# A written-out order of 2,098 parts drawn anew, and two of eight products of a matrix multiplication put last

## The chip, the cores and the metric

The kernel runs on one core of a Trainium2 chip. The metric is the device time of one execution in microseconds (us). The engines are PE (TensorE, matrix products), DVE (VectorE), ACT (ScalarE), POOL (GpSimd) and SP (SyncE); each works through its own queue of instructions in order. SP computes nothing here: it issues every transfer (DMA) of the kernel, one after the other, and waits at the head of its queue until the data of the next transfer are ready.

## The reference, cut to what matters

```python
for t in range(S):                       # S = 768, 4 batches, 8 heads, D = 40
    y[:, :, t] = einsum('bhd,bhde->bhe', r_t, state)
    Sa = einsum('bhde,bhe->bhd', state, a_t)
    state = state * w_t[:, :, None, :] - einsum('bhd,bhe->bhde', Sa, b_t) \
            + einsum('bhd,bhe->bhde', v_t, k_t)
x = y.transpose(0, 2, 1, 3).reshape(4, 768, 320)
h = maximum(x @ w_in, 0)                 # w_in: 320 x 1024
conv_out[t] = sum(conv_w[k] * h[t + k - 1] for k in range(3))
out = (h * sigmoid(conv_out)) @ w_out    # w_out: 1024 x 320
```

A recurrence over 768 time steps makes y; a product with w_in, a convolution over three time steps, a gate and a product with w_out follow.

## The kernel before

The recurrence is solved in 24 chain steps of 32 time steps each. Two chain steps form a pair, whose inputs w, a, k, b and r are loaded together; v is loaded for each step. The output goes through the second part in 12 windows of 64 time steps. The work of every step, pair and window is written as Python generators, cut by `yield` into parts, and the string `ORDER` names the parts one by one: `advance` runs a part up to its next `yield`, and so the order of the string is the order in which each engine gets its instructions. Nothing reorders them afterwards. What stands first in an engine's queue and waits holds up all that stands behind it on that engine.

The parts that matter here, by the names of their tiles (a number behind a name counts steps or pairs, for xh and xl it is the first step of the window):

- `solve_in` (pair): SP stores at, the scores of the pair, as bd in DRAM and reads it back as bb.
- `solve` (pair): 15 pairs of small operations on POOL make xx from bb (for pair 0 on DVE). SP stores xx as xd, then reads xd back as tt, and bd once more as nb. For the first two pairs SP first fills xd with zeros.
- `chain` (step): on PE pp, then pw (reads tt), pe (reads nb), pu (reads tt) and pn; between them ACT and DVE bring the results back. DVE makes the new state s, POOL makes se from it, and pp of the next step reads se.
- `finish` (step): PE turns the output (pq), DVE makes xf, ACT makes xh, POOL makes xl, the rest that xh left of xf. The 320 columns stand as three groups of 120, 120 and 80 rows, so the third group leaves 40 of 120 rows free.
- `moe_pack` (window): two transfers that move rows of xh into the free rows of the third group, of xh and of xl. `move_rows` does the same once for the weights wih and wil, and ACT then copies 80 rows of wih into wil.
- `moe_in` (window and quarter fp): for each of two column blocks j, eight products into ph; then the convolution and gate on ACT and DVE, which leave g.
- `moe_out`: po, the product of g with the weights wo.
- `weights`: 23 pieces of the weights, in 64 bits each, are loaded and changed to 32 bits by five operations on DVE and one or two each on ACT and POOL.

The eight products of a block stand in this order before (`wih[:, 2]`, `wil[:, 2]`, `xh[:, 2]` and `xl[:, 2]` hold moved rows):

```python
passes = (
    (wih[:, 0], xh[:, 0]), (wih[:, 1], xh[:, 1]), (wih[:, 2], xh[:, 2]),
    (wil[:, 0], xh[:, 0]), (wil[:, 1], xh[:, 1]), (wih[:, 0], xl[:, 0]),
    (wih[:, 1], xl[:, 1]), (wil[:, 2], xl[:, 2]),
)
```

Of the kernel before, what the change touches and what calls it, by code (L numbers as in the profile page):

```python
# [40 lines left out]
    pa0 we6 ou0 we6 we3 pa0 ch1 dd2.0 we5 ut0 we7 ut0 lv0 ut0 ch1 ld2 we7 ha3 de2.0 lr0 ha3 dd2.0
    ld3 ch1 si0 we6 lv0 so1 dd2.0 we6 ld2 so1 we8 ha3 sc2 dd2.1 so0 ch1 sc4 dd2.1 fi0 we8 ch1 dd2.1
    ch1 sc4 ch1 lr1 sc5 ut1*2 st1 lv2 pa1 ou1 dd2.0 we8 lv2 we7*2 we9*2 fi0 sc5 we8 ou1 fi0 ld3
    de3.0 lr1 we9 ch2 we10 we9 we11 we10 so1 ch2 ou1 si1 we9 we11 fi1 rt1 lv3 we10 fi1 si2 we11 ch2
    lv3 we11 fi1 we10*2 so2 si2 rt1 we12 st2 sc1 ha4 we13 de3.0 ch2 we12 ch2 we13 ld3 we8 ou2 ch2
    ut2 ch2 ut2 dd3.0 ld3 we13 we12 pa2 sc4 ou2 so2 we12 we13 we14 we15 we14 ha4 ha5 ld3 ha4 ha5 ou2
    we15 ha5 we14 dd3.0 fi2 ch3 st3 we14 ch3 dd3.0 we16 lv4 so2 we15 we16*2 de3.1 so2 ro0 we6 we15
    we17 ch3*2 lv4 ha2 de3.1 fi2 we17 ch3 fi2 so1 lr2 we17 we16 de3.1 we18 dd3.1*3 we16 ut3*2 ch3
    pa3 ch3 ld4 we18*2 we17 dd1.1 ou3 ro0 pk0 mi0.0 we19 ld4 pk0 we18*3 sc6 lr2 ou3 ro0 we17 we11
    we20 we19 sc6 sc7 we18 de4.0 fi3 so2 we19 ch4 we12 we19 mi0.0 we19 ch4 st4 lv5 mi0.0 we20 mi0.1  # L50
    we20*2 rt0 we21 we22 ld4 rt2 sc7 we17 we20 ch4 we21 we20 mi0.1 we20 rt2 mi0.0 dd1.0 ch4 de4.0
    lv5 fi3 si3 we22 fi3 ou4 ch4 de4.1 ch4*2 we19 ut4 we21 we7 so3 ut4 mi0.0 ha6 pa4 mi0.1 ou4 ld4
    ld5 pa4 de1.0 we17 mi0.2 si3 ou0 ch2 mi0.0*2 ld4 so3 ha6 mi0.1 fi3 mi0.1 ut2 mi0.0 mi0.2 mi0.0
    mi0.2 rt2 ou0 mi0.0 mi0.2 ch5 so3 lr3 ch5 ha7 sc6 so3 mi0.1 dd4.0 ha7 lv5 mo0.0 dd4.0 we19 st5
    de4.1 lr3 ch1 dd4.0 lr1 mi0.1 ch0 ch5 mi0.2 mi0.3 dd4.1*2 ch5 mi0.1*2 we21 mi0.3 dd2.1 ch1 de5.0
    mi0.3 ou5 mi0.2 ch4 we4 ch5 pk1 fi4 mi1.0 sc8 ut3 ut5 mi0.1 lv6 ld5 mi0.2*3 ld5 mi1.0 mo0.0
    de4.1 mi0.2 ch5 lv6 fi4 mi0.3 ut5 dd4.1 mi1.0 mi0.3 pa5 sc8 we5 so3 lv6 ou5 mi0.3 mi1.1 fi4 fi5
    ld5 fi4 sc9 ut4 ha8 rt3 lv1 mi0.3 sc9 st2 st1 fi5 fi4 ch5 mi0.3 ch6*2 st6 de5.0 mi0.3 mi1.0
# [93 lines left out]
def tile_decay_delta_attention_then_conv_gate_moe(  # L152
# [136 lines left out]
    wih = cp.tile([GR, G, DF], F32R, name="wih")  # L289
# [886 lines left out]
```

## Time and profile before

| what | value |
|---|---|
| time, median of 3 runs | 607.12 us (604.34 to 611.71) |
| the profiled execution | 608.01 us, of which the span of its instructions 606.3 us |
| mean granted clock of PE | 0.947 of full speed |
| PE busy | 539.3 us, 89% of the span |
| DVE, ACT, POOL busy | 395.9, 384.9 and 323.8 us |

The span runs from the first to the last instruction; 1.7 us of the execution lie outside it. PE has two clocks, 2.4 GHz (granted clock 1.00) and 1.2 GHz (0.50); a mean between them says which share of a stretch ran at which. "Issue" as the cause of a wait means that the profile shows nothing that the engine waited for.

### The profile page before, as it was taken

The page shows a single profiled execution, that of the slowest core. Times are in us where ns is not written, and L with a number is a line of the kernel's source. Part 1 is how long each engine was busy: PE and PEld are TensorE (multiplying, and loading weights), DVE is VectorE, ACT ScalarE, POOL GpSimd, SP SyncE. Part 2 cuts the span into 40 slices and gives each one's busy share as a digit, 9 for nine tenths or more (in the row PEclk, how much of TensorE's full clock was granted, in tenths as well). Part 3 has the DMA queues.
Part 4 walks back from the last instruction along what each step waited for, and adds up shares of the span by engine and source line. Part 5 has one row for each costly group of instructions (what it writes and reads, how often), then busy time and mean ns, then how long its engine had stood idle before and what let it go on. Part 6 is the DMA issues. An engine that isn't in the chain of part 4 may idle for free.

```text
span 606.3 us, 29431 instructions
## 1 busy us (share of the span) xinstructions
PE 539.3 (89%) x13021; PEld 450.5 (74%) x13021; DVE 395.9 (65%) x757; ACT 384.9 (63%) x922; POOL 323.8 (53%) x690
## 2 busy tenths in 40 slices
PE   3666776798989999989699999999999999899998
PEld 2555565686878788778588878788788887787884
DVE  7897788998796566638366476566556743654660
ACT  2354366576886776666568676857677666576561
POOL 4414886976858638556408637347538457330000
PEclk9967697898999999999989999999899999899999
DMA  9955845667345463442451357334431231200001
GB/s 149 151 108 100 153 104 113 148 133 118 64 94 87 87 119 56 87 84 45 90 89 36 65 98 130 73 69 71 90 68 36 65 54 30 58 6 27 23 27 35
DMA packets 214755, 49.11 MB, mean 81 GB/s; under 512 B 203324, under 2 KB 208404, under 8 KB 214628
## 3 DMA queue, kind: packets, MB, share of 16 engines
q1 hardware_dynamic: 214628, 47.23, 41.3%
q8 instruction: 102, 1.67, 1.2%
q14 instruction: 25, 0.20, 0.1%
HBM read 36.72 MB, written 9.18 MB: 76 GB/s over the span
## 4 chain that ended last, share of the span: by engine, by line
PE 61%; DVE 13%; ACT 10%; DMA 8%; issue 3%; POOL 3%; SPq 2%; DVEq 0%; POOLq 0%; ACTq 0%
PE po L934 15%; PE ph L889 12%; PE pm L534 3%; PE pn L724 3%; ACT vu L712 3%; PE pu L705 3%; PE ps L534 2%; PE pp L669 2%; DVE cc L918 2%; DMA bd<-at 2%; PE py L837 2%; PE pvt L787 2%; DMA xh<-xh 2%; PE pw L681 2%; PE pp L657 2%
## 5 line engine op out<-in xcount | busy, mean ns | idle before, releaser
L918 DVE SCALAR_TENSOR_TENSOR cc<-hb,cw,cc 128x256 f32<-128x256 f32 x192 | 111.3, 601 | 16.2 <-ACT cc L910 12.7
L934 PE MATMUL po<-wo,g 128*128 128x320 f32 x384 | 117.4, 443 | 0.0
L748 POOL TENSOR_TENSOR se<-s,ws 120x480 f32<-120x480 f32 x69 | 72.1, 1073 | 47.7 <-DVE s L739 29.3
L934 PEld LDWEIGHTS po<-wo,g 128*128 128x128 f32 x384 | 68.9, 192 | 22.3 <-issue 0.8
L622 POOL TENSOR_TENSOR stg<-xx,bb 128x15 f32<-128x15 f32 (+4 forms) x165 | 55.9, 339 | 27.7 <-DMA bb<-bd 16.4
L889 PE MATMUL ph<-xh,wih 120*128 120x256 f32 x288 | 57.3, 306 | 7.4 <-DMA xh<-xh 7.4
L739 DVE SCALAR_TENSOR_TENSOR s<-pn,side,s 120x240 f32<-120x240 f32 x90 | 35.8, 460 | 42.6 <-PE pn L724 42.6
L628 POOL TENSOR_TENSOR xx<-xx,stg 128x15 f32<-128x15 f32 (+4 forms) x165 | 53.4, 324 | 12.9
L712 ACT COPY vu<-pu 32x320 f32<-32x320 f32 x96 | 40.1, 418 | 23.2 <-PE pu L705 21.5
L926 DVE TENSOR_TENSOR g<-cc,hb 128x512 f32<-128x512 f32 x48 | 36.1, 755 | 23.3 <-ACT cc L923 23.3
L865 POOL TENSOR_TENSOR xl<-xf,xh 120x384 fp32r<-120x384 f32 x24 | 26.0, 1084 | 45.6 <-ACT xh L863 45.6
L889 PEld LDWEIGHTS ph<-xh,wih 120*128 120x128 f32 x288 | 41.4, 191 | 11.2 <-DMA xh<-xh 7.8
L910 ACT ACTIVATE cc<-hb,cw 128x256 f32<-128x256 f32 x96 | 43.8, 509 | 0.9 <-POOL hb L899 0.9
L800 ACT ACTIVATE sn<-pt,hmask 120x480 f32<-120x480 f32 x69 | 40.7, 665 | 3.5 <-PE pt L797 3.3
L903 ACT ACTIVATE hb<-ph 128x512 f32<-128x512 f32 x48 | 28.7, 599 | 21.1 <-PE ph L889 21.0
L923 ACT ACTIVATE cc<-cc 128x512 f32<-128x512 f32 x48 | 30.3, 635 | 17.8 <-DVE cc L918 17.7
L889 PE MATMUL ph<-xl,wih 120*128 120x256 f32 x192 | 39.0, 284 | 2.0 <-issue 2.0
L558 ACT ACTIVATE ap<-ah,hmask 120x384 f32<-120x384 f32 (+1 forms) x72 | 36.5, 574 | 6.5 <-DVE ah L513 6.4
L889 PE MATMUL ph<-xh,wil 120*128 120x256 f32 x192 | 38.7, 283 | 0.0
L493 POOL TENSOR_TENSOR ws<-wc,hmask 120x18 f32<-120x18 f32 x24 | 5.9, 247 | 59.2 <-DVE wc L489 58.9
L424 POOL COPY vu<-vin 96x240 f32<-96x240 f32 (+1 forms) x72 | 29.8, 451 | 12.7 <-DMA vin<-in_v_dram 10.6
L855 DVE TENSOR_TENSOR xf<-pq,pre 120x384 f32<-120x384 f32 x24 | 13.3, 553 | 33.1 <-PE pq L853 29.7
(310 smaller groups left out, 1281.2 us busy)
## 6 DMA issues: line engine op xcount, KB each, us to landing
inw<-in_w_dram SPq DMA_DIRECT2D x24, 160.0 KB
ina<-in_a_dram SPq DMA_DIRECT2D x24, 160.0 KB
ink<-in_k_dram SPq DMA_DIRECT2D x24, 160.0 KB
inb<-in_b_dram SPq DMA_DIRECT2D x24, 160.0 KB
rin<-in_r_dram SPq DMA_DIRECT2D x24, 160.0 KB
vin<-in_v_dram SPq DMA_DIRECT2D x48, 80.0 KB
out_dram<-ob SPq DMA_DIRECT2D x22, 160.0 KB
bd<-at SPq DMA_DIRECT2D x24, 128.0 KB
```

Of the source, the lines that this page charges most:

```text
L558: nc.scalar.activation(out=ap[:, by_set(h)], in_=ah[:, : NH[h]], func=AF.Copy, scale=hmask[:, h : h + 1])
L622: eng.tensor_tensor(t3, xx[:, 0:nj, i : i + 1].to_broadcast([128, nj, nt]), bb[:, i : i + 1, i + 1 :].to_broadcast([128, nj, nt]), ALU.mult,)
L628: eng.tensor_tensor(xx[:, 0:nj, i + 1 :], xx[:, 0:nj, i + 1 :], t3, ALU.add)
L712: nc.scalar.copy(vu[q, y, :HD], pu[y][q])
L739: nc.vector.scalar_tensor_tensor(out=dst, in0=src, scalar=side[:, x : x + 1], in1=dst if x else old[:, zs], op0=ALU.mult, op1=ALU.add,)
L748: nc.gpsimd.tensor_tensor(wide.rearrange("p b g h d -> p (b g) h d")[:, :, h], new.rearrange("p b g d -> p (b g) d"), ws[:, :, h : h + 1]. ...
L800: nc.scalar.activation(out=sn.rearrange("p b h g d -> p (b h) g d")[:, :, g], in_=pt[:GR].rearrange("p b (h d) -> p (b h) d", d=D), func=A ...
L889: nc.tensor.matmul(ph[:, j], l[:, fs], x, start=(j == 0 and i == 0), stop=(i == len(passes) - 1), skip_group_check=True,)
L910: nc.scalar.activation(out=cc[:, j], in_=hb[:, j, :, 1 : W + 1], func=AF.Copy, scale=cw[:, 1, f : f + 1],)
L918: nc.vector.scalar_tensor_tensor(out=cc[:, j], in0=hb[:, j, :, x : W + x], scalar=cw[:, x, f : f + 1], in1=cc[:, j], op0=ALU.mult, op1=ALU ...
L926: nc.vector.tensor_tensor(gt, cc, hb[:, :, :, 1 : W + 1], ALU.mult)
L934: nc.tensor.matmul(po[:rows, :DM], part(f), wo[:, f, :], start=(f == 0), stop=(f == NF - 1))
```

## The change

The string `ORDER` is replaced: the same parts in the same number, in another order, which was drawn by a planner that counts the transfers as a queue that serves one after the other. In `moe_in` the two products with moved rows come last of the eight. No operation is added or removed; the sums into ph are added up in another order. Lines behind the table are higher by one.

```diff
 ORDER = """
-    ld0*2 de0.0*2 de0.1*2 dd0.0 ld0 dd0.0 ld0 dd0.0 dd0.1 ld0 de0.0 de0.1 dd0.0 dd0.1*2 sc0 lr0*2
+    ld0 de0.0*2 de0.1 ld0 de0.0 de0.1 ld0*2 dd0.0*2 ld0 dd0.0 dd0.1 dd0.0 dd0.1 sc0 dd0.1 we0*2
...
@@ -877,9 +878,9 @@
         passes = (
-            (wih[:, 0], xh[:, 0]), (wih[:, 1], xh[:, 1]), (wih[:, 2], xh[:, 2]),
-            (wil[:, 0], xh[:, 0]), (wil[:, 1], xh[:, 1]), (wih[:, 0], xl[:, 0]),
-            (wih[:, 1], xl[:, 1]), (wil[:, 2], xl[:, 2]),
+            (wih[:, 0], xh[:, 0]), (wih[:, 1], xh[:, 1]), (wil[:, 0], xh[:, 0]),
+            (wil[:, 1], xh[:, 1]), (wih[:, 0], xl[:, 0]), (wih[:, 1], xl[:, 1]),
+            (wih[:, 2], xh[:, 2]), (wil[:, 2], xl[:, 2]),
         )
```

Three places show what the new table does. The first is SP's queue at the start, from the read of tt0 for chain step 0 on (ina, ink, inb and inw are the inputs of the next pair, wi02r and wi12r pieces of the weights). Before:

```order
L636 DMA tt0_564<-xd0_140 128x1x512
L640 DMA nb0_566<-bd0_321 128x1x512
L415 DMA ina_126<-in_a_dram 64x16x40 x2
L590 DMA xd1_141<-zero_138 1024x1x64
L595 DMA bd1_695<-at2_509 32x1024 x2
L604 DMA bb1_698<-bd1_695 64x16x16 x2
L415 DMA ink_128<-in_k_dram 64x16x40 x2
L365 DMA wi02r_845<-in_moe_w_in_dram 120x512
L365 DMA wi12r_908<-in_moe_w_in_dram 120x512
```

And in the change:

```order
L637 DMA tt0_597<-xd0_140 128x1x512
L641 DMA nb0_599<-bd0_325 128x1x512
L591 DMA xd1_141<-zero_138 1024x1x64
L596 DMA bd1_738<-at2_534 32x1024 x2
L605 DMA bb1_741<-bd1_738 64x16x16 x2
L366 DMA wi02r_828<-in_moe_w_in_dram 120x512
L366 DMA wi12r_844<-in_moe_w_in_dram 120x512
L416 DMA ina_126<-in_a_dram 64x16x40 x2
L416 DMA ink_128<-in_k_dram 64x16x40 x2
```

The load of ina has moved from ahead of the zeros and bd1 to behind both pieces of the weights, and these now come ahead of ink.

The second place is SP's queue around the moved rows of window 4 (xh8 and xl8), which stand near the solution of pair 6 (xx6, tt6, nb6). Before:

```order
L444 DMA rin_132<-in_r_dram 64x16x40 x2
L432 DMA vin_136<-in_v_dram 32x16x40 x2
L634 DMA xd0_140<-xx6_5186 64x16x16 x2
L636 DMA tt6_5785<-xd0_140 128x1x512
L640 DMA nb6_5787<-bd6_5044 128x1x512
L432 DMA vin_136<-in_v_dram 32x16x40 x2
L959 DMA out_0_dram<-ob20_5647 2x64x320
L873 DMA xh8_4868<-xh8_4868 40x256
L873 DMA xl8_4869<-xh8_4868 40x256
```

And in the change:

```order
L445 DMA rin_132<-in_r_dram 64x16x40 x2
L416 DMA inw_124<-in_w_dram 64x16x40 x2
L416 DMA ina_126<-in_a_dram 64x16x40 x2
L433 DMA vin_136<-in_v_dram 32x16x40 x2
L874 DMA xh8_4859<-xh8_4859 40x256
L874 DMA xl8_4860<-xh8_4859 40x256
L635 DMA xd0_140<-xx6_5047 64x16x16 x2
L637 DMA tt6_5878<-xd0_140 128x1x512
L641 DMA nb6_5880<-bd6_5036 128x1x512
```

The moved rows stand ahead of xd, tt6 and nb6 now, and behind two loads that came later before. Those of window 3 (xh6) move in the same way, from behind bb6 to ahead of the solution of pair 5.

The third place is PE's queue in chain step 3, at the first product of the second part (ph00). Before:

```order
L461 MATMUL pw31_1884<-ident_80,inw_124 120x128 x3
L681 MATMUL pw3_1904<-psb3_1853,tt1_1363 32x40 x32
L692 MATMUL pe3_1939<-w13_1937,nb1_1365 32x40 x32
L705 MATMUL pu30_1991<-psb3_1853,tt1_1363 32x40
L705 MATMUL pu31_1992<-psb3_1853,tt1_1363 32x40
```

And in the change:

```order
L682 MATMUL pw3_1892<-psb3_1881,tt1_1348 32x40 x32
L693 MATMUL pe3_1937<-w13_1925,nb1_1350 32x40 x32
L890 MATMUL ph00_1982<-xh0_1041,wih_152 128x256 x2
L890 MATMUL ph00_1982<-xh0_1041,wil_153 128x256 x2
L890 MATMUL ph00_1982<-xl0_1042,wih_152 128x256 x2
L890 MATMUL ph00_1982<-xh0_1041,wih_152 128x256
L890 MATMUL ph00_1982<-xl0_1042,wil_153 128x256
L706 MATMUL pu30_1991<-psb3_1881,tt1_1348 32x40
```

The eight products of the first block of window 0 stand between pe3 and pu3 now; before they came behind most of step 3. The transfers of window 0's moved rows have moved up in SP's queue as well, to right behind `move_rows`.

## Rows read from the trace of the kernel before

**Rows 1.** The page, part 1: busy time, share of the span and instructions.

```profile
PE 539.3 (89%) x13021; PEld 450.5 (74%) x13021; DVE 395.9 (65%) x757; ACT 384.9 (63%) x922; POOL 323.8 (53%) x690
```

**Rows 2.** Windows: length, busy time of each engine, granted clock, DMA share.

```profile
0.00:150.00 150.00, 103.43 (x2604) 87.91 (x2605) 124.72 (x262) 80.01 (x186) 92.81 (x206) 0.83 0.69 128
150.00:606.30 456.30, 435.84 (x10420) 362.60 (x10417) 271.21 (x496) 304.88 (x737) 231.01 (x485) 0.99 0.34 66
```

**Rows 3.** Waits of PE from 150 us: total, times, longest.

```profile
PE ph L889 <- DMA xh<-xh: 7.4, 2, 5.6
PE pp L669 <- issue: 2.8, 3, 1.3
PE ph L889 <- issue: 2.0, 1, 2.0
...
PE pe L692 <- ACT w L686: 0.2, 1, 0.2
```

**Rows 4.** Timeline of PE, the two products that waited for moved rows.

```profile
264.57 0.39 PE L889 MATMUL ph<-xh,wih 120*128 120x256 f32 x1 [1.82 <-DMA xh<-xh]
...
302.93 0.58 PE L889 MATMUL ph<-xh,wih 120*128 120x256 f32 x1 [5.56 <-DMA xh<-xh]
```

**Rows 5.** Timeline of SP's queue of transfers around the longer of these waits.

```profile
289.68 0.60 SPq L636 DMA_DIRECT2D tt<-xd  x1
...
293.59 4.42 SPq L873 DMA_DIRECT2D xh<-xh  x1
```

**Rows 6.** Chain of waits: the two transfers that ended them (start, duration).

```profile
262.16 2.36 DMA xh<-xh
...
293.59 9.30 DMA xh<-xh
```

**Rows 7.** Windows of the longer wait and of the stretch behind it.

```profile
297.30:303.00 5.70, 0.14 (x2) 0.07 (x1) 1.08 (x3) 0.63 (x1) 1.93 (x4) 0.80 0.47 105
303.00:307.50 4.50, 4.50 (x76) 3.79 (x77) 0.77 (x2) 1.23 (x3) 0.00 (x0) 0.50 0.94 151
```

**Rows 8.** Chain of waits at the start: start, duration, what.

```profile
41.51 0.64 SPq L415
...
43.95 4.75 SPq L590
...
48.80 0.60 SPq L595
...
49.44 5.02 DMA bd<-at
...
61.87 2.94 POOL se L748 x3
```

**Rows 9.** Timeline of DVE at the start: source of bd1, wait for weights.

```profile
44.30 1.28 DVE L567 TENSOR_TENSOR at<-ps,trin 128x512 f32<-128x512 f32 x2
...
62.92 1.03 DVE L300 TENSOR_SCALAR wi02q<-wi02r 120x256 int32<-120x256 int32 x1 [3.00 <-DMA wi02r<-in_moe_w_in_dram]
```

**Rows 10.** Timeline of PE, the last two products of chain step 3's solve.

```profile
114.53 0.79 PE L692 MATMUL pe<-w,nb 32*32 32x40 f32 x64 [0.70 <-ACT w L686]
116.96 1.64 PE L705 MATMUL pu<-psb,tt 32*32 32x40 f32 x64 [1.63 <-DVE psb L696]
```

**Rows 11.** Timeline of SP's queue: moved rows of weights and of window 0.

```profile
106.10 0.91 SPq L373 DMA_DIRECT2D wih<-wil  x1
...
115.24 3.02 SPq L873 DMA_DIRECT2D xh<-xh  x1
```

**Rows 12.** Window of low clock around chain step 3.

```profile
116.40:123.20 6.80, 6.22 (x111) 5.60 (x115) 6.33 (x14) 3.27 (x8) 6.17 (x17) 0.50 0.76 142
```

**Rows 13.** Chain of waits: one group of eight products at full clock.

```profile
266.26 1.13 PE ph L889 x8
```

**Rows 14.** Waits of SP's queue over the whole span.

```profile
SPq L873 <- POOL xl L865: 36.2, 2, 23.2
```

**Rows 15.** Timeline of PE: the product of step 12 that reads tt6.

```profile
309.55 0.79 PE L681 MATMUL pw<-psb,tt 32*32 32x40 f32 x64
```

More of the change, by code (lines that the diff above doesn't have):

```diff
@@ L41 @@
[L41 to L46, printed above, removed]
@@ new lines @@
+    de0.1 sc0 sc1 sc0 sc1 lv0 we1 lv0 we0*2 we1 ld1 we2 de1.0 we2 ld1 de1.0 ld1 we0 si0 so0 dd1.0
+    si0 we1 ha0*2 so0*2 we1 we2 lr0 lv0 ha1 de1.1 lr0 we3 we2 ha1 so0 we1 dd1.0 ld1 ld2 de1.1 ld1
+    ch0*2 dd1.0 lv1 dd1.1 we4 dd1.1 lr0 dd0.1 rt0 ha1 dd1.1 lv1 we3 we4 ha0 sc2*2 sc3 de2.0 de1.0
+    sc3 we3*2 we5 we4 ha2 de2.0 so0 we2 sc2 ch0 we5 ch0 de2.1 ch0 we4 we3 de2.0 de2.1 rt0 si1 ch0
+    so1 ut0*2 ha2 pa0 ch0 si1 we5 we6 so1 we5 we7 dd1.0 ou0*2 ha3 pa0 ou0 we6 ch1 ut0 we7 ut0 ch1
+    ha3 so1 ld2 ou0 ch1 we6*3 so1 ld2*2 dd2.0*2 ld2 we7 rt0 dd2.0 dd2.1 we5 fi0 pa0 ch1 lr1 we8 we7
@@ new lines @@
+    ch6 lv6 lv7 de5.0 ou6 mi1.0 de5.1 ch6 mo0.0 so3 ld5 lv7 de5.1 ha8 ut6 sc7 ut6 ch6 lv7 st1 ld5
+    pa6 mi1.1 pa6 ou6 ha9*2 mi0.3 ut6 dd5.0*2 dd5.1 fi1 dd5.0 ut6 lr3 si4 mi1.1 de5.1 mi1.1 ha9
+    dd5.1 mi1.2 mi1.0 so4 fi5 pa6 si4 ch6 ch7 sc10 fi4 ou6 lv1 mi1.0 mi1.2 we21 mo0.0 ch0 fi5 ch7
+    mi1.2 ch7 dd5.1 ch6*2 st7 mi1.0 ut6 mi1.3 ch4 lr4 mi1.1 lv8 ou6 ld6 de6.0 lv6 lr4 ch7 lv8 mo0.1
+    mi1.2 mi1.1 ld6 mi1.2 mi0.2 ch7 mi1.1 mi1.3 mi1.1 lr4 fi3 mi1.3 fi5 mi1.2 ha8 ch6 mi1.3 lv8
+    mi1.2 fi6 so4 mi1.0 ld6 mi1.1 ut7*2 dd3.0 mi1.1 lv9 ch7 sc10 sc11 sc10 pa7 sc11 fi6 ou7 lr1 ou7
@@ new lines @@
+    fi13 ch14 ut14 mi4.2 ut14 mi5.0 mi4.2 lv16 mi5.0*2 ch14 mi4.3 ha14 pa14 mi5.1 mi5.0 ld9 mi4.3
+    mi5.1*2 fi12 mi4.3 sc17 ld9 ha16 lv16 ut14 ou14 mi5.0 ch15 pa3 ch15 ha17*2 so8 lv15 ch14 mi4.3
+    dd9.0*2 mi5.0 mi5.1 dd9.1 lv16 mi4.2 lv17 mi5.2 mo3.0 mi5.0 mi5.2 mi5.0 lv16 st15 so8 mo3.1
+    dd9.1 ch14 mi5.1 ch15 mi5.1 st7 mo4.0*2 ld9 ch14 ch15 mi5.2 ch15 dd9.0 mi5.0 sc18 mi5.3 mi5.1
+    ch15 mi5.2 ut15 mi5.1 mi5.3 mi5.1 so8 mi5.1 ha17 ch13 ut15 ou15 ld10 st2 mi5.3 lv17 fi14 rt8
+    dd9.1 ch15*2 pa15 sc18 ou15 mi5.2 ld10 ch13 ch16 ha18 so8 lr1 sc19 ld10 mi5.2 de10.0 ch16 fi14
@@ new lines @@
+    mo4.0 mo3.1 st6 ld10 lv17 ou15 lv18 mi5.3 mo4.0 sc3 ou15 ch16 mi5.3 fi14 st16 fi15 lv3 ch16
+    mo4.1 de10.0 we22 de6.1 sc18 rt8 so8 mo4.1 ch16 mi5.3 mo4.1 ch16 ut16*2 pk6 mi6.0 fi14 ha16 fi14
+    mi5.3 mo2.0 pk6 de10.1 lr9 ut16 ha18 fi11 mi5.2 sc19 si9 pk5 sc19 pa16 fi15 ou16 ut16 ch16
+    ch17*2 ou16 lv18 ch16 mo4.0 mo4.1 mi5.2 ha19 mi5.3 mo4.1 mi5.2 mi6.0 de10.1 ha19 mo4.1 mi6.0
+    lv18 pa13 mi6.0 mi5.3 lr9 si9 mi6.1 ch16 so9 mi6.0 mi6.1 mi6.0 mi5.2 mi6.1 mi6.0 mo5.0 rt7 mi5.3
+    mi6.0*2 dd10.0*3 dd10.1 rt5 ch17 st17 mi5.3 dd10.1 ut11 dd10.0 so9 pa16 st6 dd10.1 lr9 ch17
@@ new lines @@
+    mo5.0 lv17 mi6.0 ch17 mi6.1 so6 mi6.1 mi6.0 rt8 mi6.0 mi6.1 mo5.0 fi13 mi6.2 so9 pa9 mi6.2
+    de10.0 lv19 sc20 ut17 dd9.1 mi6.1 ut17 mi6.2 ch17 sc20 ut15 dd7.1 st6 sc21 pa17 mi6.1 mi6.3*2
+    so9 ou17 ld11 mi6.3 fi15 fi16 ch17 fi16*2 ut16 ou17 de11.0 ch18 st18 mi6.1 ut12 mi6.2 so7 fi17
+    de11.0 fi17 ld11 de11.1 rt3 ch18 de2.1 ch14 lr10 rt8 mi6.3 pk7 fi17 mi6.2 ut13 sc11 mi6.3 lr8
+    mo4.0 mi6.3 pa8 mo5.0 mi6.1 mo5.1 de11.1 fi16 mo5.1 rt9 so9 ou13 ld10 fi17 so9 de11.0 fi16 ch18
+    fi16 rt9 fi15 pk7 de10.1 mo5.1 lv3 rt9*2 mi7.0 pa11 ch18 sc21 lv1 ch18 mi6.2 ch17 mi6.2 mo5.0
@@ new lines @@
+    mo5.1 mi6.2 ut18 mi6.3 mi6.2 mi7.0 rt9 rt8 lr10 mi7.0 dd11.0 ut18 mi7.0 ch18 ch17 mi6.3 de9.1
+    mi6.3 rt3 ha19 mi6.2 mi7.1 lv18 pa18 si10 mi7.0 ha20 sc21 lv19 mi7.1 lv20 mi7.1 ha20 mi7.1 ch15
+    ou18 de3.0 ld11 sc20 fi17 ch18 fi0 ou18 mi6.3 ha21 pa17 mi7.0 ou18 mi7.0 mo5.1 so10 mi7.2 ch19
+    lr2 ch19 ut10 ha21 mi7.0 mi7.2 mi7.1*2 mo5.0 mi7.2 mi7.0 st19 mi7.0 mi7.1 ha18 rt3 mi7.3 mi7.1
+    mi7.3 mi7.1 ha20 dd11.0 so10 ch19 rt5 ld11 dd11.0 ut18 ld11 ha21 de11.1 lv2 mi7.3 dd11.1 mo6.0
@@ new lines @@
+    lr11 ou23 pa23 mi9.3 mi10.0 ut10 mo8.1 mi10.0*2 mi9.3 ou23 rt11 mi10.0 fi22 pk9 mi10.1 rt10
+    mi10.1 mo8.0 mi10.1 mi10.0 mi10.1 fi22 mi10.0 mi10.1 fi23 st3 mo9.0 mi10.2 fi23 mi10.2 dd10.1
+    mi10.2 ou17 mi9.0 mo9.0 mi10.1*2 mi10.3 mi10.1*2 mi10.3 mo9.0 mi10.2 mi10.3 mi10.1 mi10.3 fi23
+    st4 mo9.0 fi23 pk11 st16 mi11.0 st5 mi10.2 st11 mi10.2 mi10.3*2 mi10.0 fi19 mi10.2 mi10.3
+    mo9.1*4 mi10.2 ch18 mi10.2 mi11.0 mo9.1*2 pk11 st23 mi10.2 ou23 mo9.0 ut18 mi11.0 mi10.3 mi11.1
+    mi11.0 mi11.1 mi11.0*2 mi11.1*2 st19 mi11.0 mi9.3 pa10 pa12 mi11.0 mi11.1 lv2 mi10.3 pa16 mi11.2
@@ new lines @@
+    lv21 st18 mi10.0 mi11.2*3 mi11.1 st19 pa14 ou22 mo8.0 mi11.3 mi11.1*2 mi11.3 mi11.1 mi11.2
+    mi11.3 mo10.0*5 mo10.1 mi11.3 mi11.1 mi11.2 ou16 mi11.3 mi11.2 mo10.1 ha22 mo10.1*2 st17 st21
+    mi11.2 mo10.1*2 mi11.3 mo11.0 st23 mi11.2 mi11.3*2 mo11.0*2 mi11.3 mi9.3 mo11.0 pa23 mo11.0 en0
+    st14 st9 ou21 mo11.1 ch23 mo11.1 mi11.0 mi11.3 mo11.1 pa19 mo11.0 st10 st12 mo11.1 lr1 mo11.1
+    pa7 mi10.3 ch18 st21 lr2 ou21 pa20 dd11.1 st8 st16 ou14 ou19 mo11.1 pa17 mo9.0 st6 ou17 lv23
+    st15 ut21 en0 mi11.0 we22 ut23 ha23 we22 pa18 mi11.2 en0 mo10.0 st22
```

164 lines of the change are left out of this document (62 added, 102 removed).

## The prediction, made before the change was run

> **What bounds the kernel now.** I read the page's busy times first, then windows, then PE's waits, and last the chain of waits and SP's queue at the places found. PE is busy for 539.3 of 606.3 us [rows 1], and the two windows show where it is not: up to 150 us it works 103.4 us, at a mean granted clock of 0.83, while DVE works 124.7 us; behind that it works 435.8 of 456.3 us, at 0.99 [rows 2]. So there are two kernels in one. At the start the recurrence has to come going, DVE changes weights, and PE waits for chains of other engines and transfers. From 150 us on PE is the bound, and only 20.5 us are left between its instructions; what takes work from another engine there is worth nothing, and what takes a wait from PE is worth that wait.
>
> Of these 20.5 us the two waits for moved rows are 7.4 us, the largest item. Waits with the cause "issue" are 2.8 and 2.0 us; the list goes on in small change to its last row of 0.2 us, 11 rows in all with 17.1 us [rows 3]. The rest is the end and gaps too short for that list.
>
> **The change part by part.** *The products with moved rows.* Both waits stand at the third product of a block, the first that reads a moved row: 1.82 us in window 3 and 5.56 us in window 4 [rows 4]. The chain of waits shows why they differ: the transfer that ended the first took 2.36 us from its issue, that of the second 9.30 us [rows 6]. The second was issued 3.9 us behind tt6, the issue alone held SP for 4.42 us [rows 5], and the load of the whole path behind it was shared. Putting the products last lets six of eight run first. A group of eight takes 1.13 us at full clock [rows 13], so six cover 0.85 us: of the two waits that would save 1.7 us and leave 5.7. It is the new place in SP's queue that must save the rest: both packs now stand ahead of the solution of a pair and not behind it, so that they neither wait for bd6 nor share the path with tt6 and nb6. In window 4 the cast that feeds the pack also comes a chain step earlier in ACT's queue, on average 539.3/24 = 22 us of PE's work [rows 1]. With that lead, even 9.30 us would be covered. I take the whole 7.4 us; the bounds are 1.7 (only the products' new place counts) and 7.4.
>
> *The clock behind the long wait.* In the 4.5 us that follow the wait PE is busy all the time at a granted clock of 0.50 [rows 7], its lower level. At the upper one that work takes 2.25 us, so 2.25 us go with the wait. Behind the wait of 1.82 us the products run at the full clock, so nothing is added there. Bounds 0 and 2.25.
>
> *A rule on transfers.* The row of the first wait has 2.36 us for 40 KB in a quiet stretch, that of the second 9.30 us in a full one [rows 6]. The Trainium skill says in "DMA: Bandwidth & Descriptors", section "Anatomy of one DMA — SWDGE (gpsimd) path", that a transfer has a fixed cost of about 2 us besides its bytes (it is given for transfers that GpSimd issues). By that rule 2 us would remain wherever a pack stands, and where PE comes to the products right behind the issue, the six in front would not hide it; the sum would then lose an estimated 1.2 us for each such window. No row shows a window of that kind besides window 3, and the rule cannot give the 9.30 us, which the queue made.
>
> *SP's queue at the start.* The chain of waits goes through SP here: the load of ina begins at 41.51 us, the zeros for xd1 hold SP from 43.95 us for 4.75 us, and only then is bd1 issued, at 48.80, and bd, bb and the first part of solve 1 lead to se for step 1 at 61.87 us [rows 8]. The source of bd1 was ready on DVE at 44.30 + 1.28 = 45.58 us [rows 9]. Without ina in front, bd1 can be issued up to 48.80 - 45.58 = 3.2 us earlier. The timeline of DVE has no gap ahead of that, and the change leaves its order there as it is but for a few operations, so no more is to be had. What follows would bring it too: DVE's wait of 3.00 us for wi02r [rows 9] is for a piece that now comes ahead of ink and is issued earlier as well. Both paths shift together, so this is not added. The zeros may still hold SP if tt0 and nb0 alone fill the path: then they end at about 41.51 + 4.75 = 46.3 us and 2.5 us are left. Bounds 0 (a later link, DVE with 124.7 of 150 us busy [rows 2], gives it back) and 3.2; I take 2.8. The load of ina itself now comes behind bb1 and two pieces, issued near 54 us by the same rows; PE reads it behind pw of step 1, which follows se of step 1 by some 4 us and so comes near 64 us, a margin above the longest landing of 9.30 us.
>
> *The first product of the second part.* pu of step 3 waits 1.63 us for psb from DVE [rows 10]. Eight products of window 0 now fill that place, 1.13 us at full clock and twice that at half. They are work that came later, so the wait turns into work: 1.6 us saved, if their data are there. The clock was 0.50 for the 6.8 us from 116.4 us on with PE busy 6.22 us [rows 12]; a fuller PE may keep the upper level, worth up to 3.1 us, which I count as a bound only. The lower bound is the first rival.
>
> *All the rest of the table.* I compared, for each of the 24 steps, what stands in PE's queue between the links of the chain in both orders. PE's position of each link moves by 0 to 7 us of work, mostly by under 2. From step 5 on, links with less work between them than the other engine needs are 30 before and 25 now. So the steady part should wait neither more nor less, apart from the packs. DVE, ACT and POOL are busy for 51 to 67% of that stretch [rows 2], and what moves on them hides behind PE. But a new order meets new collisions, and the old one had its largest other single wait at 2.0 us [rows 3]: I charge one of that size. Bounds: none, or three.
>
> *Sum.* 608.0 - 7.4 - 2.25 - 2.8 - 1.6 + 2.0 = 595.95 us, for an execution like the profiled one, which was 0.9 us above the median of 607.1. For the median that is 595.0 us, 2.0% less than before.
>
> **The rivals.** *The filler holds up the chain.* The last two of the eight products in front of pu3 need the moved rows of window 0, of the weights, and ACT's copy behind these. In the trace of before the pack was issued only at 115.24, 9.1 us behind the weights' rows at 106.10 [rows 11], and had 3.02 us of issue; ph00 would begin at 114.53 + 0.79 = 115.3 [rows 10]. For it: the old times would make PE wait about 5 us there. Against it: the pack now follows the weights' rows at once, near 108 us, and would be there by 112. If it is late by 5 us, this takes the 1.6 and gives back the 2.8: 595.0 + 4.4 = 599.4 us. The same time comes out if DVE gives nothing of the start back.
>
> *A wait remains at the packs.* The change would not do what it says if the packs land late all the same, say since they wait for xl on POOL. Then 5.7 us and the clock's 2.25 stay: 595.0 + 7.95 = 603 us.
>
> *A pack at the head of SP's queue holds up a solution, slower than before.* The packs of windows 3 and 4 now stand directly ahead of xd of a pair. SP waited 23.2 us once for xl at the head of its queue [rows 14], which cost nothing there. If this happens ahead of xd6, then tt6 and nb6 and all loads come late. tt6 was issued at 289.68 and read by pw of step 12 at 309.55 [rows 5, 15], of which 5.6 us were the PE wait that goes and at most 9.3 us the landing; some 5 us are slack. From there each us costs one: 23.2 - 5 = 18 us, 613 us. Against it: the cast for this pack comes a step earlier, and xl stands ahead of the last cut of the solve on POOL.
>
> *Everything fits.* No new wait, and the clock stays up in step 3: 595.0 - 2.0 - 3.1 = 590 us.
>
> **How the numbers follow.** The forecast of 595.0 us, with 592 to 598 as its own range, has 0.55; the rival of the filler or of DVE (599.4) 0.18; the wait that remains (603) 0.07; the solution held up (613) 0.05; everything fits (590) 0.15. The limit of 2%, about what a measurement of this kernel can tell from no change, lies at 595.0 and 619.2 us, and so in the middle of the forecast. Faster by over 2%: half of 0.55 and 0.15, 0.43. Slower by over 2%: the worst of the last case, or two of them, 0.03. Within 2%: 0.54. To leave out no more than 2 in 10 the range goes from 588 to 603: below it lies the part of "everything fits" with the bounds of the start used up, above it the solution held up and half of the wait that remains.
>
> **What would show it.** PE's list of waits from 150 us on should have no transfer of xh above 1 us, and the clock no half level in the middle of the span; else the first term is wrong. bd1 should be issued near 46 us and se of step 1 begin near 59; else the start is wrong. pu3 should not wait for psb, and ph00 in front of it not for a transfer. Between 150 us and the end PE should be idle for some 13 to 15 us instead of 20.5. What would make the prediction wrong most easily is a wait that no row of before has: a load of inputs that comes late now because ten other transfers stand ahead of it.

## The result, and the profile after

The changed kernel takes 589.68 us (median of 6 runs, 587.73 to 592.16), the kernel before 608.65 us (6 runs): a ratio of 0.9695, with a 95% interval of 0.9651 to 0.9738. That is 3.05% less, where 2.0% was forecast; the time lies in the range from 588 to 603, and outside the forecast's own range of 592 to 598. In microseconds that is 19.0 less, where 12.05 was forecast; the forecast started from a median of 607.1 us for the kernel before. The profiled execution took 589.18 us, its span 587.4.

The page of the changed kernel, busy times, answers to [rows 1]:

```profile
PE 529.7 (90%) x13021; PEld 439.9 (75%) x13021; DVE 387.3 (66%) x757; ACT 387.1 (66%) x922; POOL 326.3 (56%) x690
```

The windows (columns as in [rows 2]) up to 150 us, behind that, and a short one in chain step 3:

```profile
0.00:150.00 150.00, 104.43 (x2731) 87.41 (x2731) 124.19 (x270) 86.36 (x198) 96.63 (x219) 0.87 0.69 129
150.00:587.40 437.40, 425.22 (x10293) 352.51 (x10291) 263.16 (x488) 300.69 (x726) 229.65 (x471) 1.00 0.35 68
108.00:111.50 3.50, 3.28 (x78) 2.97 (x81) 3.26 (x10) 2.30 (x5) 2.95 (x9) 0.51 1.07 230
```

PE is busy for 9.6 us less though it does the same products, and idle for 9.3 us less. From 150 us on it stands for 437.40 - 425.22 = 12.2 us (20.5 before), at a granted clock of 1.00. The list of its waits from there on, first and last rows, answers to [rows 3]:

```profile
PE pu L706 <- issue: 2.5, 2, 1.6
PE py L838 <- DVE ms L814: 2.4, 2, 2.2
PE ph L890 <- issue: 1.3, 1, 1.3
...
PE pvt L788 <- ACT vu L713: 0.4, 2, 0.2
```

No wait for xh is left. SP's queue around the moved rows of window 4, which answers to [rows 5]:

```profile
277.79 0.87 SPq L874 DMA_DIRECT2D xh<-xh  x1
...
280.48 1.37 SPq L635 DMA_DIRECT2D xd<-xx  x2
284.10 0.60 SPq L637 DMA_DIRECT2D tt<-xd  x1
```

The issue of xh took 0.87 us (4.42 before), the solution (xd, then tt) follows, and PE waits for neither.

At the start, SP's queue answers to [rows 8]:

```profile
40.32 0.61 SPq L591 DMA_DIRECT2D xd<-zero  x1
46.54 0.80 SPq L596 DMA_DIRECT2D bd<-at  x2
49.02 1.79 SPq L605 DMA_DIRECT2D bb<-bd  x2
...
52.13 1.33 SPq L416 DMA_DIRECT2D ina<-in_a_dram  x2
```

The zeros hold SP for 0.61 us instead of 4.75, bd1 is issued at 46.54 and not 48.80, and bb1 2.5 us later, where it took 5.7. On POOL se of step 1 follows at 57.34 instead of 61.87, and on PE, in the second fence, pp of step 1 hardly waits for it:

```profile
57.34 3.00 POOL L749 TENSOR_TENSOR se<-s,ws 120x480 f32<-120x480 f32 x3
```

```profile
60.40 0.76 PE L658 MATMUL pp<-se,ah 120*32 120x120 f32 x24 [0.22 <-POOL se L749]
```

In chain step 3 the eight products of ph00 run behind pe, on the chain of waits at 109.50 us, and take 2.00 us and not the 1.13 of [rows 13]: the clock is at its lower level there, as the window of 3.50 us above shows. DVE's psb, which pu needs, comes at 110.67 us, behind five operations on a piece of weights:

```profile
109.50 2.00 PE ph L890 x8
```

```profile
110.67 0.54 DVE L697 SCALAR_TENSOR_TENSOR psb<-pe,half,psb 128x320 f32<-128x320 f32 x1
```

**Where the 18.9 us of span are.** The product pu of a chain step can be found in both traces, and cuts the span in stretches with the same steps. In the trace of before (start, duration), steps 5, 9 and 13:

```profile
161.23 0.79 PE L705 MATMUL pu<-psb,tt 32*32 32x40 f32 x64
...
243.11 0.79 PE L705 MATMUL pu<-psb,tt 32*32 32x40 f32 x64
...
334.66 0.79 PE L705 MATMUL pu<-psb,tt 32*32 32x40 f32 x64
```

and in the trace of the change:

```profile
155.69 0.79 PE L706 MATMUL pu<-psb,tt 32*32 32x40 f32 x64
...
239.02 0.79 PE L706 MATMUL pu<-psb,tt 32*32 32x40 f32 x64
...
320.94 0.79 PE L706 MATMUL pu<-psb,tt 32*32 32x40 f32 x64
```

The first stretch is 5.5 us shorter, the second 1.4 longer, the third, with both waits for xh, 9.6 shorter, and the last, up to the end of the span, 5.2 shorter (271.64 and 266.46). Two executions alone don't separate this from what differs from run to run. The traces of the experiments below hold each stretch several times in either order (a trace is left out of a stretch in which its kernel was edited further); the table gives means and, in brackets, lowest and highest:

| stretch | old order, us | new order, us | difference | forecast |
|---|---|---|---|---|
| start to step 5 | 161.0 (157.5 to 164.3; 5 traces) | 155.6 (154.6 to 156.8; 5) | -5.4 | -4.4 |
| step 5 to 9 | 82.7 (81.4 to 83.7; 6) | 83.0 (80.2 to 84.0; 7) | +0.3 | 0 |
| step 9 to 13 | 92.9 (91.6 to 94.0; 4) | 81.8 (80.9 to 83.1; 8) | -11.1 | -9.65 |
| step 13 to the end | 270.7 (268.6 to 272.9; 7) | 268.3 (266.5 to 270.8; 7) | -2.4 | 0 |
| a new wait, without a place | | | | +2.0 |

The sum is -18.6 us against -12.05. The forecast column has the prediction's terms where they belong: 2.8 and 1.6 us at the start, 7.4 and 2.25 us in the middle, and the new wait of 2.0 us, which had no place. Such a wait came between steps 5 and 9: py waits for ms from DVE, 2.20 us at 166.54 us in the trace of the change, and for 1.7 to 2.8 us near there in each trace that has the new order from the start past step 5. The one trace with the new order there that lacks it, of the kernel with the old start, has the shortest stretch, 80.2 us.

### The profile page after: what moved, and what is told of

The parts are those of the page before. It is cut to its first block, busy times and chain, and to the rows that moved or that the text cites. A ratio compares the mean times of both kernels' runs of the same rounds, so it can differ in the third digit from the quotient of the medians.

```text
span 587.4 us, 29435 instructions
## 1 busy us (share of the span) xinstructions
PE 529.7 (90%) x13021; PEld 439.9 (75%) x13021; DVE 387.3 (66%) x757; ACT 387.1 (66%) x922; POOL 326.3 (56%) x690
## 4 chain that ended last, share of the span: by engine, by line
PE 75%; DVE 11%; ACT 8%; issue 4%; POOL 1%; DMA 1%; SPq 0%; DVEq 0%; ACTq 0%
PE po L935 18%; PE ph L890 14%; PE ps L535 4%; PE pn L725 4%; PE pm L535 3%; PE pu L706 3%; PE py L838 3%; PE pvt L788 3%; PE pw L682 3%; PE py L827 2%; PE pp L670 2%; PE pe L693 2%; PE pp L658 2%; PE pz L580 2%; ACT vu L713 2%
## 5 line engine op out<-in xcount | busy, mean ns | idle before, releaser
L919 DVE SCALAR_TENSOR_TENSOR cc<-hb,cw,cc 128x256 f32<-128x256 f32 x192 | 105.6, 571 | 35.6 <-ACT cc L911 32.2
L935 PEld LDWEIGHTS po<-wo,g 128*128 128x128 f32 x384 | 67.6, 190 | 21.7
L890 PE MATMUL ph<-xh,wih 120*128 120x256 f32 x288 | 73.4, 313 | 0.0
L629 POOL TENSOR_TENSOR xx<-xx,stg 128x15 f32<-128x15 f32 (+4 forms) x165 | 56.6, 343 | 12.9
L890 PEld LDWEIGHTS ph<-xh,wih 120*128 120x128 f32 x288 | 48.3, 190 | 5.4 <-issue 1.4
L535 PE MATMUL ps<-ap,kt 120*64 120x96 f32 (+1 forms) x576 | 30.4, 263 | 8.7 <-DVE wi01q L305 4.9
L535 PEld LDWEIGHTS ps<-ap,kt 120*64 120x64 f32 x576 | 27.0, 153 | 12.3 <-ACT ap L559 8.7
L773 ACT ACTIVATE rp<-pr,hmask 120x384 f32<-120x384 f32 (+1 forms) x72 | 34.4, 563 | 0.9 <-PE pm L535 0.9
```

The source lines that it names most:

```text
L535: nc.tensor.matmul(ps[hs, y, pick(g), :], lhs(g, y)[:, hs], mk(pick(g), z, y), start=(g == 0 and y == 0), stop=True, skip_group_check=True,)
L629: eng.tensor_tensor(xx[:, 0:nj, i + 1 :], xx[:, 0:nj, i + 1 :], t3, ALU.add)
L890: nc.tensor.matmul(ph[:, j], l[:, fs], x, start=(j == 0 and i == 0), stop=(i == len(passes) - 1), skip_group_check=True,)
L919: nc.vector.scalar_tensor_tensor(out=cc[:, j], in0=hb[:, j, :, x : W + x], scalar=cw[:, x, f : f + 1], in1=cc[:, j], op0=ALU.mult, op1=ALU ...
L935: nc.tensor.matmul(po[:rows, :DM], part(f), wo[:, f, :], start=(f == 0), stop=(f == NF - 1))
```

## The experiments

Each was timed in five rounds beside the kernel before. The ratio is to the kernel before, for the changed kernel 0.9695 (0.9651 to 0.9738). The diffs name parts as the string does: ld loads w, a, k and b of a pair, si is solve_in, so solve, ch chain, ut the turn of v and u, ou the output, fi finish, pk moe_pack, mi moe_in, we a piece of the weights; the number is that of the pair, step, window or piece, and each token is one part. A moved part is shown with its neighbours. Of the 2,098 names in the table 261 stand for a part that has already run by then, and do nothing; from the third run on they are left out of the strings.

### The products' place alone, and the order alone

```diff
 ORDER = (the old one)
-            (wih[:, 0], xh[:, 0]), (wih[:, 1], xh[:, 1]), (wih[:, 2], xh[:, 2]),
+            (wih[:, 0], xh[:, 0]), (wih[:, 1], xh[:, 1]), (wil[:, 0], xh[:, 0]),
...
```

> The old order, and only the two products with moved rows put last of eight. Theory A (the two waits go with the packs' place in SP's queue): six products cover 0.85 us of each wait, so 1.7 us of 608.65 are saved at most, some 607 us, and a wait for xh of about 4.7 us stays in window 4, with the half clock behind it. Theory B (the products' place does it): both waits go, 7.4 us, with the clock 9.65 us, so 599 us.

Measured: 609.76 us, ratio 0.9996 (0.9959 to 1.0032). The list of PE's waits of this kernel from 150 us on still begins with xh:

```profile
PE ph L889 <- DMA xh<-xh: 6.2, 2, 4.7
```

The waits are 1.2 us shorter than in [rows 3], and the time does not show it: 1.7 us lie inside the interval, 9.65 do not. Theory B falls.

```diff
 ORDER = (the new one)
-            (wih[:, 0], xh[:, 0]), (wih[:, 1], xh[:, 1]), (wil[:, 0], xh[:, 0]),
+            (wih[:, 0], xh[:, 0]), (wih[:, 1], xh[:, 1]), (wih[:, 2], xh[:, 2]),
...
```

> The new order with the eight products in their old order. Theory A: the packs land before the third product too, so nothing is lost: 589 to 591 us, no wait for xh above 1 us. Theory B: the waits come back, 597 us or more.

Measured: 590.93 us, ratio 0.9702 (0.9653 to 0.9751), and no wait for xh in the list. The order does it all; the place of the two products is worth nothing that can be measured, with the old order or the new.

### The start alone, and all but the start

The first takes the new order up to the start of chain step 5, and then what is left of the old; the second the other way round.

```diff
-ORDER = OLD
+ORDER = NEW up to ch5 + the parts of OLD not yet run, in OLD's order
```

> The new order up to the start of chain step 5, the old one behind it, the products last in both. Theory C (the start's lead is kept to the end): the traces differ by 5.5 to 6.5 us at steps 4 and 5, so 602.5 us, and 601 with the products' place. Rival D (the lead is given back, as it fell to 2.3 us at step 7 in the trace of the change): 606 us or more.

Measured: 604.05 us, ratio 0.9900 (0.9861 to 0.9939): 6.1 us less, the lead is kept, and rival D falls.

```diff
-ORDER = OLD
+ORDER = OLD up to ch5 + the parts of NEW not yet run, in NEW's order
```

> The old order up to the start of chain step 5, the new one behind it, the products last in both. Theory C: the rest of the gain, 19 less 6, so some 596 us, with no wait for xh above 1 us and no half clock in the middle of the span. Rival D: nearly all of the gain, 590 to 592 us.

Measured: 596.00 us, ratio 0.9770 (0.9713 to 0.9828): 14.0 us less, with no wait for xh in the list. The two together make 20 us, the change 18.6: the parts add up within their intervals.

### The packs of windows 3 and 4 moved in the old order

```diff
 ORDER, around the solution of pair 5 (so5) and of pair 6 (so6):
+pk3
 so5
...
-pk3
 mi3.0
...
+fi9*2
 so6
...
+pk4
 so6
-fi9*2
...
-pk4
 mi4.0
```

> The old order with only the moved rows of windows 3 and 4 (and, for window 4, xh and xl of step 9) put ahead of the solution of pairs 5 and 6, the products last. Theory A: both waits for xh and the half clock behind the longer one go, 9.65 us, ratio 0.984, 600.5 us. Rival E (the wait moves: tt6 and nb6 come late, or the last loads ahead of the pack hold it): less than 4 us of gain, with a new wait of PE in windows 3 or 4.

Measured: 610.77 us, ratio 0.9998 (0.9958 to 1.0039). Both waits for xh are gone and two others stand in their place, the first and second of the list of PE's waits from 150 us on:

```profile
PE pp L657 <- POOL se L748: 3.9, 2, 3.7
PE pa L461 <- DMA ina<-in_a_dram: 3.6, 1, 3.6
```

The timeline of POOL and that of SP's queue show how. On POOL the rest xl waits for xh from ACT, with the last pairs of solve 6 behind it:

```profile
291.96 1.02 POOL L865 TENSOR_TENSOR xl<-xf,xh 120x384 fp32r<-120x384 f32 x1 [4.59 <-ACT xh L863]
```

```profile
293.01 0.85 SPq L873 DMA_DIRECT2D xh<-xh  x1
...
295.26 1.37 SPq L634 DMA_DIRECT2D xd<-xx  x2
300.23 0.59 SPq L636 DMA_DIRECT2D tt<-xd  x1
...
304.19 5.62 SPq L415 DMA_DIRECT2D ina<-in_a_dram  x2
```

tt6 is issued at 300.23 us and not at 289.68 [rows 5], in a trace that was only 3.8 us later at step 9, and the load of ina behind it holds up PE for 3.6 us at 314 us. This is the prediction's rival of the pack that holds up a solution, at a smaller price. The other wait, for se of step 11, is at 282 us: the first parts of solve 6 stand ahead of se on POOL and began late. That the pack of window 3, now ahead of xd5, bd6 and bb6, made them late was not shown apart. Rival E holds: moved without the rest of the new order, the packs only move the wait.

### The middle as a whole, and the new order up to its end

```diff
-ORDER = OLD
+ORDER = OLD up to ch9 + NEW up to ch13 + the rest of OLD, each without the parts already run
```

> The old order up to chain step 9 and from chain step 13 on, the new one between, with all its loads and not the packs alone; the products last. Theory A2 (the whole new queue of steps 9 to 12 takes the two waits away): both waits for xh go with the half clock behind, no other wait of PE of over 2.5 us comes in steps 9 to 12, 9.65 us, ratio 0.984. Rival E (as with the packs alone, the wait moves): under 4 us, ratio 0.994 or more.

Measured: 594.01 us, ratio 0.9791 (0.9744 to 0.9838): 12.7 us less (9.8 to 15.6), somewhat more than the 9.65 expected. The list of PE's waits from 225 to 330 us has two rows left, and this is the first:

```profile
PE pvt L787 <- ACT vu L712: 0.2, 1, 0.2
```

So what the packs did not bring by themselves, the whole new order of these steps did. Which of the loads and copies that moved with them are needed was not tried apart; the two waits of the run before point at ina and at xh from ACT.

```diff
-ORDER = OLD
+ORDER = NEW up to ch13 + the parts of OLD not yet run, in OLD's order
```

> The new order up to chain step 13, the old one behind it; the products last. Theory A2: start and middle together, 6.1 + 9.65 us, some 594 us, ratio 0.974, and what is left to the change's 0.9695 are the two half levels and the waits that the old order has in steps 18 and 22 (1.7 and 1.5 us, 1.6 and 2.0 us). Rival M (those come and go from run to run): 0.969 to 0.971.

Measured: 593.53 us, ratio 0.9753 (0.9699 to 0.9807): 15.0 us less. It is as theory A2 has it, but the interval reaches to the changed kernel's ratio. What the new order brings behind step 13 is -3.5 us by the two ratios and -2.4 by the traces, and not told apart from nothing by the times.

### The packs put back in the new order

```diff
 ORDER, the new one:
-pk3
 so5
...
+pk3
 mi3.0
...
-pk4
 so6
...
+pk4
 mi4.0
```

> The new order, only the packs of windows 3 and 4 put back to directly ahead of their first moe_in part, behind the solutions. Theory A (the packs' place is needed): PE comes to the moved rows within 1 us of the issue, waits 1.5 to 8 us in each of the two windows, with half clock behind, ratio 0.975 to 0.985. Rival L (the loads around them are what counts, and a pack lands at once in the new queue): ratio 0.969 to 0.972, waits for xh under 1.5 us in all.

Measured: 606.07 us, ratio 1.0008 (0.9974 to 1.0043). All of the gain in time is gone, twice what theory A allowed. First the list of PE's waits from 150 us on, then the two transfers on the chain of waits, then the two windows of half clock behind them:

```profile
PE ph L890 <- DMA xh<-xh: 10.0, 2, 6.5
```

```profile
256.04 8.16 DMA xh<-xh
...
299.30 5.43 DMA xh<-xh
```

```profile
259.90:270.10 10.20, 5.86 (x83) 5.25 (x83) 1.96 (x4) 3.54 (x9) 4.30 (x12) 0.50 0.54 100
304.20:311.00 6.80, 6.23 (x84) 4.54 (x88) 0.58 (x1) 2.17 (x5) 0.97 (x3) 0.50 0.04 11
```

With 10.0 us of waits and 5.86 + 6.23 us of work at half clock, which at full clock takes half of that, 10.0 + 6.0 = 16.0 us are lost. Steps 9 to 13 take 97.1 us in this trace, 15.3 more than the mean of the new order. The lead of the start is still there at step 9 (pu at 236.31 us, 243.11 before); steps 9 to 13 lose more than the new order had gained in them, since 97.1 us is also 4.2 above the mean of the old order. The place of the packs is needed; it is only not enough.

### The loads of ina and ink at the start

```diff
 ORDER, the old one:
-ld2
 ch0*2
...
 si1
...
-ld2
 ut0*2
...
 we6
+ld2*2
```

> The old order with only the loads of ina and ink of pair 2 put behind bd1, bb1 and wi02r; the products in their old order. Theory F (SP's queue at the start is the start's gain): the zeros hold SP for 0.6 us instead of 4.75, bd1 is issued near 46.5 us, se of step 1 begins near 57.5, and 4 to 6 us are saved, ratio 0.990 to 0.993. Rival G (the lead is given back by a later link, or by ink coming late): se comes early, and the time stays within 1.5 us.

Measured: 607.95 us, ratio 0.9946 (0.9913 to 0.9978): 3.3 us less. SP's queue and POOL's se:

```profile
40.43 0.61 SPq L590 DMA_DIRECT2D xd<-zero  x1
45.86 0.80 SPq L595 DMA_DIRECT2D bd<-at  x2
50.07 1.32 SPq L604 DMA_DIRECT2D bb<-bd  x2
```

```profile
57.33 3.03 POOL L748 TENSOR_TENSOR se<-s,ws 120x480 f32<-120x480 f32 x3 [0.22 <-DVE s L739]
```

se begins as early as in the changed kernel. Theory F holds for the place and the size. That the time is 0.7 us short of its 4 lies inside the interval, and so does what else the new start may bring.

### ph00 put back

```diff
 ORDER, the new one:
-mi0.0
 ch3
...
 ou3
+mi0.0
```

> The new order, only the eight products of ph00 put back from ahead of pu of step 3 to behind the chain's products of that step. Theory H (they fill a wait, 1.6 us, at the full clock): 1 to 2 us more than the changed kernel's 589.7, ratio to the kernel before 0.972. Rival I (they stood at half clock and held up pu as long as they filled): no change, 0.969 to 0.970, or somewhat faster.

Measured: 593.01 us, ratio 0.9698 (0.9652 to 0.9744). No difference from the changed kernel; 1 to 2 us are less than the two intervals can tell. The table's first stretch is 155.8 us in this trace, inside that of the new order. For the term of 1.6 us nothing speaks here.

### Work in PE's waits at the start

```diff
+    def warm():
+        t = psM.tile([128, 512], F32, tag="M", name="warm")
+        for count in (40, 24, 10, 20, 5):
+            for i in range(count):
+                nc.tensor.transpose(t[:, 128 * (i % 4) : 128 * (i % 4) + 128], ident, ident)
+            yield
```

The five parts stand behind pp of step 0, ahead of the first scores of pair 1, ahead of pu of steps 0 and 2, and ahead of pw of step 3.

> The new order with 99 products of the identity added that nobody reads, in PE's waits of the first 107 us, so that PE is busy there (some 16 us of work at full clock in 21 us of waits). Theory J (the half clock of the start costs time on the path): the half level, 37.7 us in the trace of the change, falls to under 20, and the time falls by 3 to 8 us, ratio 0.957 to 0.965. Rival K (DVE and the transfers set the start, and PE's clock there costs nothing): the half level may fall, the time stays, 0.967 to 0.972, or grows where the added products hold up the chain.

Measured: 591.31 us, ratio 0.9678 (0.9637 to 0.9719). The windows of this kernel, up to 150 us and from 40 to 50 us:

```profile
0.00:150.00 150.00, 112.84 (x2819) 96.11 (x2820) 124.65 (x267) 84.49 (x196) 95.72 (x214) 0.92 0.67 128
40.00:50.00 10.00, 6.03 (x196) 5.12 (x195) 9.38 (x21) 5.59 (x13) 2.71 (x6) 1.00 0.38 105
```

The mean clock up to 150 us rises from 0.87 to 0.92, and from 40 to 50 us, where the source of bd1 is made, from 0.67 to 1.00. The half levels in the span fall from 37.5 us to 27.5, not below the 20 of theory J. The time does not follow: the ratio is lower by 0.0017, 1.0 us, well inside the intervals. DVE's timeline shows why in that place: the source of bd1 is made at

```profile
45.54 1.28 DVE L568 TENSOR_TENSOR at<-ps,trin 128x512 f32<-128x512 f32 x2
```

and so is ready at 46.82 us, 0.3 us later than in the changed kernel (45.82 + 0.69 = 46.51), though PE had its products ready earlier. There DVE waited 0.45 us for PE, and that is all that a faster PE can give in this place; here DVE waits for no product, but comes to it 0.85 us later, since it had waited 0.94 us for bb at 28.55 us. Rival K holds for the 10 us at half clock that went; what the 27.5 us that stayed cost is not tested.

### One piece of weights later on DVE

```diff
 ORDER, the new one:
 ch0
-we5
 ch0
...
 ch0
+we5
```

> The new order, only the change of the weights' piece wi21 on DVE (2.1 us, ahead of psb of step 0) put behind the new state of step 0. Theory N (with SP's queue free, DVE is what sets se of step 1): psb and the state come 2 us earlier, se of step 1 begins near 55.5 us instead of 57.3, ratio 0.966. Rival O (DVE gives it back with the next pieces, or xx of pair 1 on POOL sets se): se moves by under 1 us or the ratio stays at 0.969 to 0.971.

Measured: 595.92 us, ratio 0.9821 (0.9775 to 0.9866), 7.7 us slower than the change. psb and the state did come 1.4 to 1.7 us earlier. But the piece has an addition on POOL, ahead of xx of pair 1, which moved along in the order and now waited for DVE:

```profile
56.87 0.72 POOL L315 TENSOR_TENSOR wi21q<-wi21q 80x256 f32<-80x256 f32 x1 [4.76 <-DVE wi21q L312]
...
60.68 3.24 POOL L749 TENSOR_TENSOR se<-s,ws 120x480 f32<-120x480 f32 x3
```

```profile
63.98 1.30 PE L658 MATMUL pp<-se,ah 120*32 120x120 f32 x24 [4.79 <-POOL se L749]
```

```profile
57.90:71.60 13.70, 8.62 (x206) 7.28 (x194) 7.64 (x12) 4.12 (x11) 12.21 (x28) 0.50 0.85 142
```

se of step 1 begins 3.3 us late, PE waits 4.79 us for it, and 8.62 us of work behind run at half clock. Neither theory had this: the miss is the edit's, of a step whose POOL instruction was not counted. It still gives the price of se at this place: 3.3 us of it cost 4.6 us up to step 5 in the trace (160.2 against the mean of 155.6).

## Why the prediction was right, and where not

*What bounds the kernel* was read rightly in the main: of the 18.6 us in the table 16.5 came in the two stretches with the places named, and 2.4 behind step 13, at no place named.

*The two waits for moved rows* (7.4 us) and *the clock behind the longer* (2.25 us): right in mechanism and nearly in size, 9.65 us forecast, 11.1 measured between steps 9 and 13. The trace that the forecast was read from and that of the change differ by 9.6 us there; the mean of the old order is higher because three of its four traces have 10.2 us at half clock around the longer wait, and the trace of before only 6.8. Four runs carry the mechanism. The products' place alone does nothing, the order without it everything, the packs put back take the gain of these steps away, and the middle of the new order alone brings 12.7 us. The step "the new place in SP's queue must save the rest" was right but too short: that place in the old order brings nothing, since the pack then stands ahead of a solution that is late. In that run xh came late from ACT (xl waited 4.59 us for it), and so did the load of ina (PE waited 3.61 us for it). The prediction named the cast a step earlier and two loads ahead, and did not see that such a lead is a condition. The third rival, the solution held up, was a true danger; the new order avoids it by having the pack ready: window 4's was issued at 277.79, 0.22 us behind the end of xl on POOL (276.56 + 1.01).

*Quiet and full* were read into [rows 6] without a row that shows it. While the transfer of 2.36 us ran the DMA share was 0.65, during that of 9.30 us 0.46. Why the second took four times as long is open.

*SP's queue at the start* (2.8 us): right at its first links, bd1 at 46.54 for the 46 forecast. In the pair of traces se came at 57.34, 4.5 us earlier than before, where 2.8 would have given 59. Only the time of issue was counted, but bd1 also landed sooner: bb1 was issued 2.5 us behind it instead of 5.7. But the trace of before has a late start: over five traces of the old start and six of the new the mean of se is 60.8 and 57.7 us, 3.1 apart, and so the term was near. Where only ina and ink were moved bb1 came 4.2 us behind bd1, and se came as early all the same, at 57.33, waiting for DVE's state: that is the link that is late next. In time that edit alone is worth 3.3 us (1.3 to 5.3), the whole new start 6.1 (3.7 to 8.5); whether the rest of the new start adds anything is not told apart.

*ph00* (1.6 us): its links are as forecast. pu3 does not wait for psb, and ph00 not for a transfer: its pack was issued at 100.50 us. The size is not shown. The products ran at half clock, DVE's psb was ready at 110.67 + 0.54 = 111.2 us, nearly as late as the products, and putting them back costs nothing that can be measured. The first rival, the filler that holds up the chain, did not come.

*All the rest of the table, and the new wait of 2.0 us*: this is the step that failed, and the main reason why the gain is 6.6 us larger than the forecast. It granted the redraw no gain outside the places examined, and charged it one collision. The collision came, py for ms between steps 5 and 9, but that stretch is only 0.3 us longer with it. PE is idle for 12.2 us behind 150 us instead of the 13 to 15 forecast. From step 13 on the traces of the new order are 2.4 us shorter in the mean, where nothing was forecast. PE's waits from step 13 on, first in the trace of before, then two rows of the trace of the change, show where:

```profile
PE pp L669 <- issue: 2.4, 2, 1.3
PE ph L889 <- issue: 2.0, 1, 2.0
```

```profile
PE ph L890 <- issue: 1.3, 1, 1.3
...
PE pp L670 <- issue: 0.3, 1, 0.3
```

Over the seven traces of either order PE stands for 8.9 us there in the old and 7.4 in the new, so that 1.6 of the 2.4 us are waits; pp with the cause "issue" has 1.9 and 0.4 us. Half levels come in some traces of either order (four of the old, three of the new) and do not explain it: traces without one have 269.3 us in the mean in the old order and 267.3 in the new, traces with one 271.7 and 269.6. Why pp waits less in the new order is open; no run tried it.

*The rival that fits everything* (590) has the measured time, but by luck: there was a new wait, and the clock did not stay up in step 3 (0.51). What made up for them came in part from behind step 13, where it had nothing.

*The rule on transfers* from the Trainium skill could not show itself. By "DMA: Bandwidth & Descriptors", section "Anatomy of one DMA — SWDGE (gpsimd) path", a transfer would keep about 2 us however early its place (it is given for transfers that GpSimd issues; here SP does). In the new order PE nowhere comes to the products right behind the issue. Where the packs were put back it did, and the transfers took 8.16 and 5.43 us, far more than the rule's fixed part; what set them is not shown.

## What to carry to other kernels

A wait of the bounding engine for a transfer that is issued late is worth itself and, behind most of the long ones here, half of the time that the next work took at half clock; a change of the consumer's order buys at most what the work put in between covers. Moving the transfer up an in-order queue pays only when its data are ready there: count what each moved step puts on every queue, its copies on other engines too, since twice here an early or late step passed its wait on to a solution behind it. And before filling a wait or raising a clock at a place, look which engine has the last word there; at this start it was mostly DVE and SP, and 10 us less at half clock on PE brought nothing that could be measured.

## What the hardware showed that was not expected

The old start does not repeat itself: in five traces of the same order se of step 1 begins between 58.6 and 62.2 us, with the zeros holding SP for 4.02 to 4.75 us and bb1 issued 4.2 to 5.7 us behind bd1. In the new order, with ina behind, six traces that keep its start have 57.3 to 58.3 us and 2.4 to 2.6 us. A part of the gain at the start is that the late cases are gone. The times lie closer together as well, 587.73 to 592.16 us after and 604.34 to 611.71 before; that this comes from the start is not shown, since the kernel with the new start alone ranges from 598.91 to 607.69.
